# Linear attention and a Mish MLP on one core: the first 16 slots written anew

## The chip, the cores and the metric

The kernel runs on one core of a Trainium2 chip. The metric is the device time of one execution in microseconds (us), the median of several runs. A profile of one execution gives the spans of the engines: TensorE (PE, with its weight loads as PEld), VectorE (DVE), ScalarE (ACT), GpSimd (POOL) and SyncE (SP), which issues most DMAs.

## The reference

Softmax attention without a score matrix, followed by an MLP with a Mish activation, in float32:

```python
# q, k, v: (8 batches, 8 heads, 576 tokens, 64)
q_s = softmax(q, over the 64 features)
k_s = softmax(k, over the 576 tokens)
kv  = einsum('bhsd,bhse->bhde', k_s, v)      # 64 x 64 per head
att = einsum('bhsd,bhde->bhse', q_s, kv)
x   = att as (4608 tokens, 512)
h   = x @ w_in                               # 512 -> 2048
g   = h * tanh(log(1 + exp(h)))              # Mish
out = g @ w_out                              # 2048 -> 512
```

The MLP weights arrive as float64 and are converted on the chip from their two 32-bit halves.

## The kernel before

**Items and slots.** The attention is cut into 32 items of two heads each (four items per batch). An item gives `xs[i]`, 128 features of x for 512 tokens as a rounded part and a remainder, and a tail of 64 tokens that goes through DRAM. The MLP is cut into 144 slots: nine chunks of 512 tokens (eight batches and the collected tails) by 16 blocks of 128 of the 2048 hidden features. A slot `n` has an `H` part, 12 matmuls of 128x512 (four feature blocks `t` by three products of rounded parts and remainders), Mish (`Y`), a rounded copy `gh` (`G` on DVE or `GA` on ACT), a remainder `gl` (`GL`), and three slots later an `O` part of 12 matmuls into four accumulators `po`.

**Weight units.** 32 units (16 blocks of `w_in`, 16 of `w_out`) are loaded raw (`R`) and converted in steps: `RA` scales the high half on ACT into `wc`, `RL` scales the low half on ACT in place (`RM` does it on DVE), `RB` and `RC` combine the bits and the sign on DVE, `RH` rounds on ACT into the `wih` or `wo` tile, and `RO` (POOL) or `RD` (DVE) forms the remainder.

**An item, step by step.** `LQ LK L V` load q, k transposed, k and v. `MQ`, `SQ`/`SD` take q's maximum and subtract it, `EQ` is the exponential, `Q` the sums and their reciprocals, `QM`/`QD` the product. `MK`, `B` find k's maximum and bring it across the partitions by a PE transpose, `KS` subtracts, `EK` is the exponential. `K` is the `kv` product (`pkv`), `S` and `SA`/`SB` scale it into the block-diagonal 128x128 tile `kvbd`. `T` and `TC` transpose q, `X` makes `px` (512 tokens) and `pxt` (the tail), `Z`, `ZL` give `xs`, `ZT`, `ST` store the tail.

**Order.** Inside the first 16 slots the order on all engines is written out by hand in the string `FIRST`: each token is one step, and each engine executes its instructions in the order of the tokens. `STAGED` names the buffer that each raw weight unit uses. The first 16 slots contain items 0 to 7, all weight units, `H` of slots 0 to 15 and `O` of slots 0 to 12. From slot 16 on the loop `group` issues four slots at a time and one item per four slots; there items go two by two (`a_pair`, `a_kv2`, `a_x2`), with kv as 64x64 tiles in `kvt`, each product in its own quarter of the PE array.

**Memory.** PSUM has eight banks of 128x512 float32: four (`o0` to `o3`) for `po`, and for early items; two (`h`) for the `H` sums `ph`; two (`a`) for the rest. `y`, Mish's result, goes to a buffer in SBUF. `wc` has four buffers.

```python
first = FIRST.split()                       # order of the first 16 slots
...
pkv[j * D:(j + 1) * D, 0:D + 2] += r["ke"][:, c, j].T @ r["v"][:, j, c, :]
```

Of the kernel before, what the change touches and what calls it, by code (L numbers as in the profile page):

```python
# [18 lines left out]

FIRST = (  # L20
# [27 lines left out]
def attn_mish_mlp(ctx: ExitStack, tc: tile.TileContext, q, k, v, wu, qs, kt, out):  # L48
# [4 lines left out]
    HP, D = 4, v.shape[-1]  # L53
# [65 lines left out]
    def w_low(j):  # L119
        low = conv[j][0]  # L120
        nc.scalar.activation(low, low, AF.Copy, scale=0.93 * 2.0 ** -29)  # L121

    def w_low_v(j):
        low = conv[j][0]
        nc.vector.tensor_scalar(low, low, 0.88 * 2.0 ** -29, 0.45, ALU.mult, ALU.add)

    def w_bits(j):
        low, high, a = conv[j]
        nc.vector.scalar_tensor_tensor(a, a, 3, low, ALU.logical_shift_left, ALU.bitwise_or)

    def w_sign(j):
        low, high, a = conv[j]
        nc.vector.scalar_tensor_tensor(a, high, 0x80000000, a, ALU.bitwise_and, ALU.bitwise_or)
# [25 lines left out]
    vt = [p.tile([P, 2, NC + 1, D + 2], F32, tag=f"v{j}", name=f"v{j}") for j, p in enumerate((pp, pp, pp, lp))]


    for t in vt:
        nc.gpsimd.memset(t[:, :, :, D:D + 2], 1.0)
        nc.gpsimd.memset(t[ST:P, :, NC, D:D + 2], 0.0)

    def k_load(i):
        if i >= NITEM:
            return
        r = at[i] = at.get(i, {})
        t = r["k"] = (pp if i < 3 else lp).tile([P, 2, NC + 1, D], F32, tag=f"k{min(i, 3)}", name=f"k{i}")  # L170
        nc.sync.dma_start(t, k[i])  # L171
# [9 lines left out]
    def q_load(i):  # L181
        if i >= NITEM:
            return
        r = at[i] = at.get(i, {})
        if i >= COLS:
            t = r["q"] = lp.tile([P, NB, 32], F32, tag="q3", name=f"q{i}")
            nc.sync.dma_start(t, qs[i].rearrange("p (n f) -> p n f", f=32))
            return
        t = r["q"] = (pp if i < 3 else lp).tile([P, 2, NC + 1, D], F32, tag=f"q{min(i, 3)}", name=f"q{i}")
        nc.sync.dma_start(t, q[i])  # L190

    def v_load(i):
# [33 lines left out]
    def a_qmax(i):  # L226
# [21 lines left out]
    def psum(i, tag, name):  # L248

        if i < HP and tag != "a":  # L250
            return (ps_h if tag == "h" else ps_o).tile([P, 512], F32, tag=tag, name=name)
        return ps_a.tile([P, 512], F32, tag="a", name=name)

    def a_kmax(i):
        r = at[i]
        pb = ps_a.tile([P, 512], F32, tag="a", name=f"pb{i}")
# [3 lines left out]
    def a_ksub(i):  # L260
# [4 lines left out]
        nc.vector.tensor_tensor(r["k"], r["k"], mb.unsqueeze(2).to_broadcast([P, 2, NC + 1, D]), ALU.subtract)  # L265

    def a_exp(i, which="kq"):
# [3 lines left out]
        for nm in which:  # L271
            if nm == "q" and i >= COLS:
                e = r["qe"] = ap.tile([P, NB, 32], F32, tag="qe", name=f"qe{i}")
                nc.scalar.activation(e, r["q"], AF.Exp)  # L274
                continue
            if i > COLS and i % 2:
                e = pools["ke"]
            else:
                e = (pp if i in (0, 2) else ap).tile([P, NC + 1, 2, D], F32, tag=f"{nm}e", name=f"{nm}e{i}")
            nc.scalar.activation(e.rearrange("p c h d -> p h c d"), r[nm], AF.Exp)  # L280
            r[nm + "e"] = e

    def a_kv(i):
        if i >= NITEM:
            return
        r = at[i]
        pkv = psum(i, "o0", f"pkv{i}")
        for c in range(NC + 1):
            for j in range(2):
                nc.tensor.matmul(pkv[j * D:(j + 1) * D, 0:D + 2], r["ke"][:, c, j], r["v"][:, j, c, :],  # L290
                                 start=c == 0, stop=c == NC)
# [35 lines left out]
    def a_qt(i):  # L327
# [14 lines left out]
        pq = psum(i, "o1", f"pq{i}")  # L342
        for c in range(NC):
            nc.tensor.transpose(pq[:, c * P:(c + 1) * P], r["qe"][:, c].rearrange("p h d -> p (h d)"), ident)
        pq2 = psum(i, "o2", f"pqt{i}")
# [16 lines left out]
    def a_x(i):  # L362
        r = at[i]
        px = psum(i, "o3", f"px{i}")
        nc.tensor.matmul(px, kvbd[i in (1, 3) or i >= HP], r["qT"][0], start=True, stop=True)  # L365
        r["px"] = px
        a_tail1(i)
# [4 lines left out]
    def a_x2(e):  # L372
        r1, r2 = (ps_h.tile([P, 512], F32, tag="h", name=f"pt{e}_{j}") for j in range(2))
        px = [ps_a.tile([P, 512], F32, tag="a", name=f"px{e + j}") for j in range(2)]
        pt = r1[:, 0:ST], r2[:, 2 * (D + 2):2 * (D + 2) + ST]
        for dst, x in ((pt, 1), (px, 0)):
            for j in range(2):
                for h in range(2):
                    a, b = slice(h * D, (h + 1) * D), slice((h ^ j) * D, ((h ^ j) + 1) * D)
# [267 lines left out]
```

## Time and profile before

| | before |
|---|---|
| median of 3 runs | 869.4 us (868.26 to 869.88) |
| the profiled execution's own time | 868.84 us |
| its span | 867.0 us |
| granted TensorE clock, mean | 0.998 |
| PE / DVE / ACT / POOL busy | 846.7 / 474.1 / 337.1 / 92.4 us |
| DMA | 69.16 MB, 73975 packets, 52928 of them under 512 B |

How to read profile rows: a group row has the line and engine, the operation, `out<-in` with the shapes (partitions x elements), the count, then busy us and the mean ns of one, then the engine's idle time before such instructions and what ended it. A timeline row has start, length, the instruction, and in brackets the idle time before it with its releaser. `L97` is a helper that subtracts; its rows are told apart by engine and tile.

### The profile page before, as it was taken

How to read it: one execution, taken by the hardware profiler on the slowest of the kernel's cores; microseconds unless marked ns; L12 is line 12 of the kernel's file. 1: busy time of each engine (PE TensorE's matmuls, PEld its weight loads, DVE VectorE, ACT ScalarE, POOL GpSimd, SP SyncE). 2: the span in 40 equal slices, each digit the busy share in tenths (PEclk: the TensorE clock that was granted, in tenths of full speed). 3: DMA queues.
4: the chain of work that ended last, by engine and by line, in shares of the span. 5: the costliest groups of instructions: out<-in, count | busy, mean ns of one | idle time of the engine just before them, and what ended most of it. 6: DMA issues, size and time to landing. Idle time of an engine off the chain costs nothing.

```text
span 867.0 us, 11466 instructions
## 1 busy us (share of the span) xinstructions
PE 846.7 (98%) x4368; PEld 684.3 (79%) x4368; DVE 474.1 (55%) x1196; ACT 337.1 (39%) x509; POOL 92.4 (11%) x91
## 2 busy tenths in 40 slices
PE   5999999999999999999999999999999999999998
PEld 3677778787878878787878787878788788888886
DVE  7999998555574647464655656564743222222221
ACT  4999874424352434333342434243432111111111
POOL 4024221111111110111110011111110000000000
PEclk9999999999999999999999999999999999999999
DMA  9985345312321213212231223122100020001001
GB/s 307 396 263 190 106 117 136 77 28 62 92 74 46 73 48 107 62 57 63 92 77 42 69 70 83 37 62 74 62 18 1 15 73 13 1 0 50 1 1 49
DMA packets 73975, 69.16 MB, mean 80 GB/s; under 512 B 52928, under 2 KB 52928, under 8 KB 73920
## 3 DMA queue, kind: packets, MB, share of 16 engines
q1 hardware_dynamic: 73600, 67.91, 26.5%
q8 instruction: 34, 0.56, 0.3%
q10 hardware_dynamic: 320, 0.52, 0.2%
q14 instruction: 21, 0.17, 0.1%
HBM read 57.93 MB, written 10.49 MB: 79 GB/s over the span
## 4 chain that ended last, share of the span: by engine, by line
PE 89%; ACT 6%; SPq 1%; DVE 1%; issue 1%; DMA 1%; DVEq 0%; ACTq 0%
PE po L510 43%; PE ph L465 42%; PE pt L392 2%; PE px L380 1%; DMA kt<-in_kt_dram 1%; ACT L485 1%; ACT raw_out L121 1%; ACT wc_out L117 1%; ACT raw_in L121 1%; ACT y L485 0%; PE px L365 0%; ACT L280 0%; ACT wo L146 0%; SPq L171 0%; ACT wih L146 0%
## 5 line engine op out<-in xcount | busy, mean ns | idle before, releaser
L465 PE MATMUL ph<-xs,wih 128*128 128x512 f32 x1152 | 358.4, 392 | 2.5 <-ACT y L485 2.5
L510 PE MATMUL po<-wo,gh 128*128 128x512 f32 x1152 | 355.3, 389 | 0.3 <-POOL wo L97 0.3
L465 PEld LDWEIGHTS ph<-xs,wih 128*128 128x128 f32 x1152 | 213.9, 188 | 49.1 <-ACT y L485 3.8
L510 PEld LDWEIGHTS po<-wo,gh 128*128 128x128 f32 x1152 | 216.1, 188 | 45.6 <-POOL wo L97 0.6
L485 ACT ACTIVATE y<-ph 128x512 f32<-128x512 f32 x144 | 86.2, 599 | 370.0 <-PE ph L465 310.4
L465 PE MATMUL ph<-xs,wil 128*128 128x512 f32 x576 | 224.7, 390 | 0.2 <-DVE wil L97 0.2
L510 PE MATMUL po<-wo,gl 128*128 128x512 f32 x576 | 224.1, 389 | 0.0
L490 DVE CAST gh<-y 128x512 fp32r<-128x512 f32 x132 | 60.0, 455 | 270.9 <-ACT y L485 270.7
L465 PEld LDWEIGHTS ph<-xs,wil 128*128 128x128 f32 x576 | 108.1, 188 | 23.9 <-DVE wil L97 1.0
L510 PEld LDWEIGHTS po<-wo,gl 128*128 128x128 f32 x576 | 108.1, 188 | 22.5 <-DVE gl L97 0.2
L97 DVE TENSOR_TENSOR gl<-y,gh 128x512 fp32r<-128x512 f32 x144 | 100.9, 702 | 11.9
L485 ACT ACT_TABLE_LOAD x41 | 52.6, 1283 | 72.7 <-PE ph L465 72.6
L309 POOL TENSOR_TENSOR qe<-qe,qs 128x576 f32<-128x576 f32 (+1 forms) x31 | 37.0, 1192 | 304.7 <-DVE qs L304 287.1
L97 POOL TENSOR_TENSOR q<-q,qm 128x576 f32<-128x576 f32 (+1 forms) x30 | 35.8, 1194 | 198.4 <-DVE qm L224 186.5
L280 ACT ACT_TABLE_LOAD x29 | 37.2, 1283 | 6.0 <-DMA q<-in_q_dram 3.9
L300 DVE TENSOR_REDUCE qs<-qe 128x18 f32<-128x576 f32 (+1 forms) x32 | 24.6, 768 | 26.3 <-ACT qe L274 25.2
L446 DVE TENSOR_TENSOR xs<-px,xs 128x512 fp32r<-128x512 f32 x32 | 20.9, 685 | 17.0 <-ACT xs L443 17.0
L233 DVE TENSOR_REDUCE qm<-q 128x18 f32<-128x576 f32 (+1 forms) x32 | 24.4, 763 | 4.0 <-DMA q<-in_q_dram 3.7
L515 DVE COPY ob<-po 128x512 f32<-128x512 f32 x16 | 11.1, 692 | 26.7 <-PE po L510 26.7
L203 DVE TENSOR_REDUCE mxd<-kt 128x1 f32<-128x576 f32 x32 | 23.9, 746 | 0.5 <-DMA kt<-in_kt_dram 0.4
L209 DVE STREAM_TRANSPOSE mb<-mxd 32x32 f32<-32x32 f32 x96 | 19.5, 203 | 3.1
L443 ACT CAST xs<-px 128x512 fp32r<-128x512 f32 x32 | 17.7, 591 | 7.2 <-PE px L380 7.2
(94 smaller groups left out, 503.4 us busy)
## 6 DMA issues: line engine op xcount, KB each, us to landing
k<-in_k_dram SPq DMA_DIRECT2D x32, 320.0 KB, 2.9
kt<-in_kt_dram SPq DMA_DIRECT2D x32, 288.0 KB, 2.9
raw_in<-in_w_dram SPq DMA_DIRECT2D x16, 512.0 KB, 7.7
raw_out<-in_w_dram SPq DMA_DIRECT2D x16, 512.0 KB, 4.9
out_dram<-ob SPq DMA_DIRECT2D x32, 256.0 KB, 2.2
q<-in_qs_dram SPq DMA_DIRECT2D x24, 288.0 KB, 3.0
v<-in_v_dram SPq DMA_DIRECT2D x20, 320.0 KB, 4.5
v_odd<-in_v_dram SPq DMA_DIRECT2D x12, 320.0 KB, 4.6
```

Of the source, the lines that this page charges most:

```text
L97: eng.tensor_tensor(out, a, b, ALU.subtract)
L203: nc.vector.tensor_reduce(mxd, r["kt"], axis=AX.X, op=ALU.max)
L209: nc.vector.transpose(mb[h, h], mxd[h].to_broadcast([32, 32]))
L233: nc.vector.tensor_reduce(qm, qt, axis=AX.X, op=ALU.max)
L280: nc.scalar.activation(e.rearrange("p c h d -> p h c d"), r[nm], AF.Exp)
L300: nc.vector.tensor_reduce(z, q2, axis=AX.X, op=ALU.add)
L309: eng.tensor_tensor(q2, q2, z.unsqueeze(2).to_broadcast(list(q2.shape)), ALU.mult)
L446: nc.vector.tensor_tensor(xs[i][:, 1], src, xs[i][:, 0].bitcast(F32), ALU.subtract)
L465: nc.tensor.matmul(gs[n], wi[a][:, t, fs], x[:, z], start=t == 0 and i == 0, stop=t == HP - 1 and i == 2)
L485: nc.scalar.activation(y, gs[n], AF.Mish)
L490: copy(hi, gs[n])
L510: nc.tensor.matmul(po[t], g[a][:, t * P:(t + 1) * P], wo[f][:, z], start=f == 0 and i == 0, stop=f == NF - 1 and i == 2)
```

## The change

The change replaces the hand-written order of the first 16 slots and, with it, these steps:

- PSUM is one pool of eight named banks `a` to `h`. A token of `FIRST` can name its bank or banks (`H0e`, `RL2a`, `T1ae`); an `H` without one takes `g` and `h` in turn. `po` uses `a` to `d`.
- `RL` writes the scaled low half into a PSUM bank instead of in place; `RB` combines into that bank; `RC` writes the result to `wc`. `RM` is gone; all 32 units use `RL`.
- For 20 of the 32 units the rounding is a DMA issued by POOL from `wc` to the weight tile (`RI`) instead of the ACT copy (`RH`). The remainder is formed on POOL for 27 units (14 before) and on DVE for 5 (18 before).
- In the first 16 slots Mish overwrites its PSUM bank; `G`/`GA` and `GL` read it from there. `G` is on DVE 12 times and on ACT 4 times (4 and 12 before).
- Items 4 to 7 go two by two with `kvt` and 64x64 products (`KP`, `S`, `XT`, `XP`), with k's maximum and q's transposes still on PE. Each group of four heads from batch 1 on (before: batch 2) is laid out in another order.
- v is laid out with d outermost, as `[P, D + 2, 2, NC + 1]`; the `kv` matmuls read it with a step of 10 elements, and its DMA writes one contiguous run per partition. q and k have the chunk ahead of the head.
- The exponentials of items 0 to 7 are in place. `Q` is split into `Q` and `QZ`, which adds 1e-9 with an accumulator output and takes the reciprocal; `qm`, `qs`, `rs` have two buffers.
- Items 0 to 3 are taken in the order 0, 1, 3, 2 at the end of their chains, and all four `X` stand ahead of the first `H`.

The core of the diff (the new order shown by its beginning):

```diff
 FIRST = (
-    "LQ0 LK0 L0 V0 LQ1 LK1 MQ0 LQ2 MK0 SQ0 L1 B0 V1 EQ0 KS0 LK2 LQ3 Q0 EK0 L3 K0 V2 MQ1 QM0 L2 MK1 LK3 SQ1 T0 S0 V3 "
...
+    "LQ0 LK0 L0 LQ1 L1 V0 LK1 MQ0 LQ2 V1 MK0 SQ0 LQ3 LK2 B0a L2 KS0 EQ0 L3 MQ1 LK3 V2 SD1 V3 EK0 R0 Q0 R1 EQ1 K0a "
+    "LQ4 MK1 R2 QZ0 R3 Q1 QM0 B1b L4 R4 S0 MQ2 R5 SA0 T0cd R6 MQ3 SQ2 R7 R8 TC0 KS1 R9 SQ3 QZ1 EQ2 R10 X0ab MK2 R11 "
+    "EK1 R12 QM1 MK3 EQ3 R13 Q2 R14 K1c Z0 R15 Q3 ZT0 ST0 ZL0 B3b B2d S1 T1ae RL0f QZ3 SA1 QZ2 QM3 KS2 RA0 TC1 KS3 "
+    "QM2 T3cd EK2 RB0 X1ab LQ5 EK3 MQ4 RL1e RC0 SQ4 RA1 K3f TC3 RB1 RI0 K2g V4 S3 Z1 RC1 L5 SA3 T2cd ZL1 RI1 ZT1 "
+    "RA2 ST1 X3be S2 TC2 SB2 RL2a X2cd RD0 Z3 RB2 ZT3 EQ4 ST3 H0e PP ZL3 LK4 Z2 RO1 H1 V5 RC2 ZT2 RL3b ST2 ZL2 L6 "
...
+    ps = ctx.enter_context(tc.tile_pool(name="ps", bufs=1, space=bass.MemoryType.PSUM))
+    def bank(letter, name, dtype=F32):
+        return ps.tile([P, 512], dtype, tag=f"bank_{letter}", name=name)
...
-    def w_low(j):
+    def w_low(j, b):
         low = conv[j][0]
-        nc.scalar.activation(low, low, AF.Copy, scale=0.93 * 2.0 ** -29)
+        conv[j][0] = bank(b, f"low{j}", U32)
+        nc.scalar.activation(conv[j][0], low, AF.Copy, scale=0.93 * 2.0 ** -29)
...
-        nc.vector.scalar_tensor_tensor(a, a, 3, low, ALU.logical_shift_left, ALU.bitwise_or)
+        nc.vector.scalar_tensor_tensor(low, a, 3, low, ALU.logical_shift_left, ALU.bitwise_or)
...
-        nc.vector.scalar_tensor_tensor(a, high, 0x80000000, a, ALU.bitwise_and, ALU.bitwise_or)
+        nc.vector.scalar_tensor_tensor(a, high, 0x80000000, low, ALU.bitwise_and, ALU.bitwise_or)
...
+    def w_hi_dma(j):
+        a, d = w_dst(j)
+        nc.gpsimd.dma_start(d[0], a.bitcast(F32R))
...
+        t = pool.tile([P, D + 2, 2, NC + 1], F32, tag=tag, name=f"{tag}_0")
...
-                nc.tensor.matmul(pkv[j * D:(j + 1) * D, 0:D + 2], r["ke"][:, c, j], r["v"][:, j, c, :],
+                nc.tensor.matmul(pkv[j * D:(j + 1) * D, 0:D + 2], r["ke"][:, c, j], r["v"][:, :, j, c],
...
+    def a_qinv(i):
+        q2, z = at[i]["z"]
+        total = ap.tile([P, 1], F32, tag="total", name=f"total{i}")
+        nc.vector.tensor_scalar(z, z, 1e-9, 0.0, ALU.add, ALU.add, accum_out=total)
         nc.vector.reciprocal(z, z)
...
+    def a_x2(e, px, pt, order):
+        for x, j, h in order:
+            a, o = slice(h * D, (h + 1) * D), slice((h ^ j) * D, ((h ^ j) + 1) * D)
+            nc.tensor.matmul((px, pt)[x][h][o], kvt[a, j], at[e + j]["qT"][x][a], start=True, stop=True)
...
+    def g_mish0(n):
+        nc.scalar.activation(gs[n], gs[n], AF.Mish)
```

More of the change, by code (lines that the diff above doesn't have):

```diff
@@ L155, in attn_mish_mlp, with v_tile @@
     xs = {}
-    ap.tile([P, 32], F32, tag="gap0", name="gap0")
+    ap.tile([P, 96], F32, tag="gap0", name="gap0")
     xt_dram = dp.tile([B, P, HP, ST], F32, name="xt_dram")
[L159 to L164, printed above, removed]
+    def v_tile(pool, tag):
+        t = pool.tile([P, D + 2, 2, NC + 1], F32, tag=tag, name=f"{tag}_0")
+        nc.gpsimd.memset(t[:, D:D + 2], 1.0)
+        nc.gpsimd.memset(t[ST:P, D:D + 2, :, NC], 0.0)
+        return t
+    vt = [v_tile(p, f"v{j}") for j, p in enumerate((pp, pp, pp, lp))]
     def k_load(i):
@@ L246, in a_qm, with a_kmax @@
         a_qsub(i)
[L248 to L254, printed above, removed]
+    def a_kmax(i, b):
         r = at[i]
-        pb = ps_a.tile([P, 512], F32, tag="a", name=f"pb{i}")
+        pb = bank(b, f"pb{i}")
         nc.tensor.transpose(pb[:, 0:P], r["mxd"].to_broadcast([P, P]), ident)
@@ L271, in a_exp, with a_kv @@
         for nm in which:
[L272 to L277, printed above, removed]
-            else:
-                e = (pp if i in (0, 2) else ap).tile([P, NC + 1, 2, D], F32, tag=f"{nm}e", name=f"{nm}e{i}")
-            nc.scalar.activation(e.rearrange("p c h d -> p h c d"), r[nm], AF.Exp)
+            if i < COLS:
+                e = r[nm]
+            elif nm == "q":
+                e = ap.tile([P, NB, 32], F32, tag="qe", name=f"qe{i}")
+            else:
+                e = pools["ke"] if i % 2 else ap.tile([P, NC + 1, 2, D], F32, tag="ke", name=f"ke{i}")
+            nc.scalar.activation(e, r[nm], AF.Exp)
             r[nm + "e"] = e
-    def a_kv(i):
-        if i >= NITEM:
-            return
+    def a_kv(i, b):
         r = at[i]
-        pkv = psum(i, "o0", f"pkv{i}")
+        pkv = r["pkv"] = bank(b, f"pkv{i}")
         for c in range(NC + 1):
             for j in range(2):
-                nc.tensor.matmul(pkv[j * D:(j + 1) * D, 0:D + 2], r["ke"][:, c, j], r["v"][:, j, c, :],
+                nc.tensor.matmul(pkv[j * D:(j + 1) * D, 0:D + 2], r["ke"][:, c, j], r["v"][:, :, j, c],
                                  start=c == 0, stop=c == NC)
-        r["pkv"] = pkv
     def a_qsum(i):
@@ L318, in a_kvs @@
         pkv, rs = at[i]["pkv"], at[i]["rs"]
-        bd = kvbd[i in (1, 3) or i >= HP]
+        bd = kvbd[i % 2]
         for j in range(2):
@@ L360, in a_qt2, with a_x, a_xt, a_xp @@
         r["qT"] = qT, qTt
[L362 removed]
+    def a_x(i, b):
         r = at[i]
[L364 to L379, printed above, removed]
[L380 to L387 removed]
+        px, px2 = bank(b[0], f"px{i}"), bank(b[1], f"pxt{i}")
+        nc.tensor.matmul(px, kvbd[i % 2], r["qT"][0], start=True, stop=True)
+        nc.tensor.matmul(px2[:, 0:ST], kvbd[i % 2], r["qT"][1], start=True, stop=True)
+        r.update(px=px, pxt=px2[:, 0:ST])
+    def a_x2(e, px, pt, order):
+        for x, j, h in order:
+            a, o = slice(h * D, (h + 1) * D), slice((h ^ j) * D, ((h ^ j) + 1) * D)
+            nc.tensor.matmul((px, pt)[x][h][o], kvt[a, j], at[e + j]["qT"][x][a], start=True, stop=True)
+        for j in range(2):
+            at[e + j].update(dict(px=px[j]) if px else {}, **dict(pxt=pt[j]) if pt else {})
+    def a_xt(e, b):
+        a_x2(e, None, [bank(b[j], f"pt{e + j}")[:, 0:ST] for j in range(2)], [(1, j, h) for j in range(2) for h in range(2)])
+    def a_xp(e, b):
+        a_x2(e, [bank(b[j], f"px{e + j}") for j in range(2)], None, [(0, j, h) for j in range(2) for h in range(2)])
+    def a_xpair(e):
+        r1, r2 = (turn_bank(f"pt{e}_{j}") for j in range(2))
+        px = [bank("ef"[j], f"px{e + j}") for j in range(2)]
+        a_x2(e, px, (r1[:, 0:ST], r2[:, 2 * (D + 2):2 * (D + 2) + ST]),
+             [(x, j, h) for x in (1, 0) for j in range(2) for h in range(2)])
+        return r2
+    def a_kv2(e, pkv):
         for i in range(e, e + 2):
@@ L414, in a_pair @@
             a_tail3(e + 1)
-        if pkv is not None:
-            a_kvs2(f, pkv)
-    def a_tail1(i):
-        r = at[i]
-        px2 = r["pxt"] = psum(i, "a", f"pxt{i}")
-        nc.tensor.matmul(px2[:, 0:ST], kvbd[i in (1, 3) or i >= HP], r["qT"][1], start=True, stop=True)
+        if f < NITEM:
+            a_kvs2(f)
     xt_first = []
@@ L433, in a_tail2 @@
         at[i]["xt"] = xt
-        nc.scalar.copy(xt, at[i]["pxt"][:, 0:ST])
+        nc.scalar.copy(xt, at[i]["pxt"])
     def a_tail3(i):
@@ L631 @@
         "in_k_dram": rows(k, N, True),
-        "in_v_dram": rows(v, N, False),
+        "in_v_dram": rows(v, N, False).transpose(0, 1, 4, 3, 2),
         "in_w_dram": _np.ascontiguousarray(units).view(_np.int64),
```

129 lines of the change are left out of this document (69 added, 60 removed), and 36 rows, old and new, of the table FIRST.

## The prediction

> **What bounds the kernel now.** I read first the page's busy shares, then the busy time by stretch, then the PE's timeline and the chain through the end of the first 16 slots. The page:
>
> ```profile
> PE 846.7 (98%) x4368; PEld 684.3 (79%) x4368; DVE 474.1 (55%) x1196; ACT 337.1 (39%) x509; POOL 92.4 (11%) x91
> ```
>
> These are averages over stages with different limits. The busy time in three stretches (columns: stretch, its length, then busy us with counts on PE, PE's weight load, DVE, ACT, POOL, then clock, DMA share and GB/s), cut at the first `H` matmul (26.0 us) and at the first matmul of slot 16 (125.4 us):
>
> ```profile
> 0.00:26.00 26.00, 15.30 (x116) 10.87 (x117) 19.16 (x42) 15.05 (x32) 11.10 (x22) 0.93 1.01 324
> 26.00:125.40 99.40, 94.14 (x475) 72.31 (x474) 93.65 (x161) 90.31 (x161) 26.70 (x22) 1.00 0.63 207
> 125.40:310.30 184.90, 184.90 (x1027) 150.04 (x1026) 113.18 (x331) 71.48 (x96) 18.59 (x16) 1.00 0.28 76
> ```
>
> In the middle stretch three engines are nearly full at once: PE 95%, DVE 94%, ACT 91%. POOL is at 27%. After it PE alone is full, DVE at 61%, ACT at 39%. The chain and the PE timeline of that later part:
>
> ```profile
> 128.30 2.72 PE po L510 x12
> ...
> 213.91 2.96 PE ph L465 x12
> ...
> 260.12 2.96 PE ph L465 x12
> ...
> 141.83 0.81 PE L392 MATMUL pkv<-v,ke 128*64 128x66 f32 x20
> ...
> 143.15 0.73 PE L465 MATMUL ph<-xs,wih 128*128 128x512 f32 x2
> ```
>
> Twelve matmuls take 2.72 us, 227 ns each. The period of eight slots is 260.12 - 213.91 = 46.21 us, of which 16 x 2.72 = 43.52 are slot matmuls; 2.69 are one pair of items. Its `kv` half is 143.15 - 141.83 = 1.32 and the `x` half the remaining 1.37. There is no gap: what the PE has to do there sets the end. So the change can gain only ahead of 125.4 us, and it can lose behind it only by making a PE instruction slower. Every us by which slot 16 starts earlier is a us of the end.
>
> **What the middle stretch loses now.** PE timeline rows (start, length, operation, idle before and its releaser):
>
> ```profile
> 26.01 0.71 PE L465 MATMUL ph<-xs,wih 128*128 128x512 f32 x2
> ...
> 34.33 0.73 PE L465 MATMUL ph<-xs,wih 128*128 128x512 f32 x2 [1.13 <-ACT y L485]
> ...
> 55.27 0.81 PE L290 MATMUL pkv<-v,ke 128*64 128x66 f32 x20
> 56.00 0.74 PE L465 MATMUL ph<-xs,wih 128*128 128x512 f32 x2
> ...
> 61.24 0.33 PE L346 MATMUL pqt<-ident,qe 128*128 128x128 f32 x1 [1.64 <-ACT qT L358]
> ...
> 64.86 1.02 PE L365 MATMUL px<-qT,kvbd 128*128 128x512 f32 x2
> ...
> 65.85 0.70 PE L465 MATMUL ph<-xs,wih 128*128 128x512 f32 x2
> ...
> 73.87 0.60 PE L344 MATMUL pq<-ident,qe 128*128 128x128 f32 x4
> ...
> 74.33 0.71 PE L465 MATMUL ph<-xs,wih 128*128 128x512 f32 x2
> ...
> 109.91 0.73 PE L465 MATMUL ph<-xs,wih 128*128 128x512 f32 x2 [1.35 <-ACT y L485]
> ...
> 125.42 0.62 PE L465 MATMUL ph<-xs,wih 128*128 128x512 f32 x2
> ```
>
> PE's necessary work from 26.0 to 125.4: 16 `H` and 13 `O` blocks, 29 x 2.72 = 78.9. Items 4 to 7 one by one: `kv` 0.73 (56.00 - 55.27), transposes 0.46 (74.33 - 73.87), `x` with tail 0.99 (65.85 - 64.86), 2.18 each, 8.7 for four. Item 3's `x`, which lies behind the first `H`, 1.0. Sum 88.6. The stretch lasts 99.4, so 10.8 are lost: 5.3 as idle (99.40 - 94.14) and the rest in matmuls that wait for weights or run in broken sequences. Each large gap shown was ended by ACT: its queue, not its result, is late. That is what less work on ACT and DVE could give back.
>
> **The change part by part**, from rows of 0 to 125.4 us (count | busy, mean ns):
>
> ```profile
> L129 DVE SCALAR_TENSOR_TENSOR wc_out<-wc_out,raw_out 128x512 uint32<-128x512 uint32 x16 | 13.3, 856 | 0.7 <-ACT wc_out L117 0.6 <-ACT raw_out L121 0.2
> L129 DVE SCALAR_TENSOR_TENSOR wc_in<-wc_in,raw_in 128x512 uint32<-128x512 uint32 x16 | 12.7, 793 | 0.7 <-ACT raw_in L121 0.4 <-issue 0.3
> ...
> L146 ACT CAST wih<-wc_in 128x512 fp32r<-128x512 f32 x16 | 9.8, 617 | 2.5 <-DVE wc_in L133 2.5
> ...
> L121 ACT ACTIVATE raw_in<-raw_in 128x512 uint32<-128x512 uint32 x13 | 8.8, 678 | 0.0
> ...
> L97 POOL TENSOR_TENSOR wil<-wc_in,wih 128x512 fp32r<-128x512 f32 x6 | 8.1, 1356 | 16.0 <-ACT wih L146 16.0
> L280 ACT ACT_TABLE_LOAD x6 | 7.7, 1283 | 4.0 <-DMA q<-in_q_dram 3.9
> ...
> L490 ACT CAST gh<-y 128x512 fp32r<-128x512 f32 x12 | 7.3, 618 | 0.0
> ...
> L97 DVE TENSOR_TENSOR wil<-wc_in,wih 128x512 fp32r<-128x512 f32 x10 | 7.0, 707 | 1.0 <-ACT wih L146 0.8
> ...
> L446 DVE TENSOR_TENSOR xs<-px,xs 128x512 fp32r<-128x512 f32 x8 | 5.4, 679 | 0.2 <-ACT xs L443 0.2
> ...
> L323 ACT ACTIVATE kvbd<-pkv,rs 64x64 f32<-64x64 f32 x12 | 3.7, 311 | 5.2 <-DVE rs L315 5.1
> ...
> L97 DVE TENSOR_TENSOR q<-q,qm 128x640 f32<-128x640 f32 x2 | 1.6, 816 | 0.0
> ...
> L125 DVE TENSOR_SCALAR raw_in<-raw_in 128x512 uint32<-128x512 uint32 x3 | 1.3, 428 | 0.0
> ```
>
> *ACT.* The rounding of 20 of 32 weight units moves from ACT to a POOL-issued DMA (`RI` for `RH`): -20 x 0.617 = -12.3. `gh` copies on ACT fall from 12 to 4: -8 x 0.618 = -4.9. The scaled `kvbd` copies fall from 12 to 6: -6 x 0.311 = -1.9. Five `RM` become `RL` on ACT: +5 x 0.678 = +3.4. Exp and Mish alternate 14 times in the new order instead of 12: +2 x 1.283 = +2.6. Sum -13.1.
>
> *DVE.* `RD` falls from 18 to 5: -13 x 0.707 = -9.2. `RM` goes: -5 x 0.43 = -2.1. `RB` reads one operand from PSUM; its mean is stretched by POOL now, as these rows show:
>
> ```profile
> 22.31 0.69 DVE L129 SCALAR_TENSOR_TENSOR wc_in<-wc_in,raw_in 128x512 uint32<-128x512 uint32 x1
> ...
> 31.30 1.32 DVE L129 SCALAR_TENSOR_TENSOR wc_in<-wc_in,raw_in 128x512 uint32<-128x512 uint32 x1 [0.35 <-ACT raw_in L121]
> ...
> 30.77 1.30 POOL L97 TENSOR_TENSOR wil<-wc_in,wih 128x512 fp32r<-128x512 f32 x1 [8.50 <-ACT wih L146]
> ```
>
> The same instruction takes 0.69 with POOL idle and 1.32 inside a POOL subtraction. The nearest row with one SBUF and one PSUM input is `xs<-px,xs`, 0.679. I take that: -32 x (0.825 - 0.679) = -4.7; ends 0 and -5. [...] The twelve `gh` copies on DVE read PSUM now; I bound them by today's 455 ns for the SBUF form on the page and 0.692 for the `ob<-po` copy:
>
> ```profile
> L490 DVE CAST gh<-y 128x512 fp32r<-128x512 f32 x132 | 60.0, 455 | 270.9 <-ACT y L485 270.7
> ...
> L515 DVE COPY ob<-po 128x512 f32<-128x512 f32 x16 | 11.1, 692 | 26.7 <-PE po L510 26.7
> ```
>
> Taken at 0.692, the PSUM form: 12 x 0.692 - 4 x 0.455 = +6.5. Two fewer `q` products and subtractions on DVE: -1.6. The pairwise `kvbd` scaling and the accumulator outputs of `QZ` I put at +0.5 together. Sum -10.6.
>
> *POOL.* `RO` rises from 14 to 27, +13 x 1.356 = 17.6; `SQ` and `QM` gain two instructions, priced like the same subtraction, 2.7; and 20 DMA issues whose price no row shows. From 26.70 in the middle stretch POOL goes to 47.0 plus 18 issues (two lie ahead). [...] I take 1.0, so 65 of some 91 us.
>
> *PE.* Items 4 to 7 in pairs: 2 x 2.69 + 4 x 0.46 = 7.2 instead of 8.7. Item 3's `x` is ahead of the first `H` in the new order: -1.0. Necessary work 78.9 + 7.2 = 86.1.
>
> *The first `H`.* It moves behind `X2`. DVE has more ahead of it: `MQ4` and `SD1`, about 2 x 0.82, less two `RM`, 0.86; +0.8. In return the `v` loads have contiguous rows:
>
> ```profile
> k<-in_k_dram SPq DMA_DIRECT2D x32, 320.0 KB, 2.9
> ...
> v<-in_v_dram SPq DMA_DIRECT2D x20, 320.0 KB, 4.5
> ```
>
> The same 320 KB should then land in 2.9 instead of 4.5 us, and three `v` loads stand ahead of item 3's `kt` now. But DVE is busy 19.16 of the first 26 us, and its first 3.85 go to the first load, so little of it reaches the path. Against it stands `RI0`: a DMA in place of a 0.62 us cast, 1 us of issue and some 2.9 of landing, as for `k`, mostly under `X3` and `X2`. I put the first `H` at 27.0, ends 25 and 30.
>
> *Mish in PSUM, the pinned banks.* Mish, `G` and `GL` hold a bank longer, and four banks carry `ph`, `low` and items 4 to 7. No row prices it. A wait for a bank would stand on ACT's queue in front of the next Mish, for which PE waits: 0 to the whole present loss.
>
> *`v` with d outermost.* PE's streamed operand of the 320 `kv` matmuls steps 10 elements (40 bytes) instead of 1. Twenty passes of 66 columns take 0.66 us (half of 1.32) with both column halves at work together, so each half reads 66 columns per 66 ns, 1.0 a nanosecond, where a slot matmul reads 512 per 227, 2.25. A read at half rate (1.13) would still feed one half, but not two through one port. Ends: 0, and 2.0/1.13 = 1.77 times as long, +0.51 us per item. I take 0, since the stream asks for less than half of what the slot matmuls draw. [...]
>
> **Sum.** ACT falls to about 77 and DVE to 83 in the stretch, PE to 86.1: PE leads again, by little. I let half of the present loss stay, 5.4, since all three are still near 90% full and `RI` is slower than a cast. Slot 16 starts at 27.0 + 86.1 + 5.4 = 118.5 instead of 125.4: -6.9. The profiled run took 868.84 (span 867.0, 1.84 around it); 868.84 - 6.9 = 861.9. The median of the runs is 869.4, 0.6 above it. Forecast 862; with the loss at 2 and the first `H` at 25 it is 856.5, with 9 and 28 it is 866.5.
>
> **The rivals.** (1) *Strided `v`: slower.* At +0.51 per item the 24 items behind slot 16, where nothing hides PE time, cost 12.2, the eight ahead up to 4: 862 + 12.2 + 4 = 878. It passes today's time from +0.23 per item on. For it: the step; against it: the low rate of the stream. Chance 0.14.
> (2) *POOL becomes the bound.* Above (86.1 + 5.4 - 47)/18 = 2.5 us per issue POOL's in-order queue sets the pace, and `RO` behind a waiting `RI` delays weights for PE. At 3 us POOL alone needs 101 and slot 16 starts at 128: 871. Against it: 73% of POOL is free now, in waits for ACT's casts. Chance 0.14, on both sides of today's time.
> (3) *Banks take back the gain.* ACT and DVE get lighter, but waits for banks keep the loss at 10 to 11: 867 to 869. Chance 0.13; the change then hardly shows.
> (4) The forecast, 856 to 866: chance 0.59.
>
> A measurement here tells some 0.2% (1.7 us) from no change. From the cases: faster 0.68 (0.59, half of 3, a little of 2), same 0.13, slower 0.19 (most of 1, half of 2). Range 855 to 873: it holds cases 2 to 4 and leaves out strided `v` in full.
>
> **What would show it.** Slot 16's first matmul near 118.5 and the first `H` near 27; ACT and DVE below 90% between; `RB` near 0.68 with POOL busy; POOL's issues near 1 us; 46.21 us for eight slots as before, and 1.32 for a pair's `kv`. A longer period means rival 1; POOL above 90% rival 2; PE waiting for `y` while ACT waits for DVE's `gl` or `wc` rival 3.

## The result and the profile after

| | before | after |
|---|---|---|
| median | 868.83 us (868.25 to 869.88, 4 runs) | 907.47 us (905.14 to 907.74, 4 runs) |
| profiled execution, its span | 868.84, 867.0 us | 907.27, 905.5 us |
| ratio, 95% interval | | 1.0438 (1.0424 to 1.0451) |
| first `H` matmul, first matmul of slot 16 | 26.01, 125.42 us | 34.57, 149.51 us |
| period of eight slots, `kv` of a pair | 46.21, 1.32 us | 47.41, 2.53 us |

The forecast was 862 us, in the range 855 to 873. The kernel became 4.4% slower. From the page after, its span and busy shares:

```profile
span 905.5 us, 11577 instructions
...
PE 865.5 (96%) x4384; PEld 699.7 (77%) x4384; DVE 460.8 (51%) x1212; ACT 327.6 (36%) x482; POOL 123.2 (14%) x126
```

DVE and ACT have less work, as was meant, and PE is busy for longer. The same three stretches as before, cut again at the first `H` and at slot 16 (same columns):

```profile
0.00:34.57 34.57, 16.05 (x120) 11.19 (x121) 19.88 (x49) 18.03 (x38) 11.92 (x23) 0.96 0.99 365
34.57:149.51 114.94, 97.92 (x484) 74.43 (x485) 80.23 (x148) 79.72 (x128) 56.73 (x56) 0.94 0.65 192
149.51:334.40 184.89, 184.89 (x979) 150.40 (x979) 109.97 (x330) 68.00 (x91) 18.57 (x16) 1.00 0.24 71
```

In the middle stretch no engine is full any more: PE 85%, DVE and ACT 70%, POOL 49%. They wait for one another, as the list of waits below shows, and the clock is 0.94. In the last stretch PE is full and at full clock, as before. The chain there shows what has changed in it:

```profile
191.64 2.53 PE pt L416 x40
194.17 2.94 PE ph L486 x12
...
239.05 2.53 PE pt L416 x40
241.58 2.94 PE ph L486 x12
```

The slot matmuls are what they were (2.72 for twelve, 2.94 behind a pair), but the pair's `kv` takes 2.53 instead of 1.32. The period is 241.58 - 194.17 = 47.41.

So two losses add up: slot 16 starts 149.51 - 125.42 = 24.1 later, and twelve pairs behind it cost 12 x 1.21 = 14.5 more. 38.6 against the span's 905.5 - 867.0 = 38.5. Where the first of them begins is in the PE timeline and, below it, in POOL's:

```profile
27.62 0.33 PE L385 MATMUL pxt<-qT,kvbd 128*128 128x64 f32 x2
34.57 1.19 PE L486 MATMUL ph<-xs,wih 128*128 128x512 f32 x2 [6.62 <-DMA wih<-wc_in]
...
43.19 1.22 PE L486 MATMUL ph<-xs,wih 128*128 128x512 f32 x2 [5.73 <-DMA wih<-wc_in]
```

```profile
23.12 0.94 POOL L162 DMA_DIRECT2D wih<-wc_in  x1
34.75 0.77 POOL L162 DMA_DIRECT2D wih<-wc_in  x1 [10.69 <-issue]
...
43.29 2.52 POOL L111 TENSOR_TENSOR wil<-wc_in,wih 128x512 fp32r<-128x512 f32 x2 [7.49 <-DMA wih<-wc_in]
```

`RI0` is issued at 23.12, before anything waits for it, and `H0` can start only at 34.57: the rounding landed 11.3 us after its issue. DVE's timeline has `RC1`, which makes the second unit's `wc`, at 24.28, over at 24.95; yet `RI1` is issued at 34.75, when the first rounding is through, after 10.69 us that the profile puts down to nothing but the issue itself. PE then waits a second time. The DMAs issued from 20 to 50 us, and the landing times of all `wih` roundings before slot 16:

```profile
GB/s 399 412 392 410 425 393 404 426 404 393 372 385 382 391 380 396 393 407 427 399 415 426 426 399 396 336 340 372 356 352 390 394 351 293 44 10 0 82 268 358
...
raw_in<-in_w_dram SPq DMA_DIRECT2D x4, 512.0 KB, 11.6
wih<-wc_in POOLq DMA_DIRECT2D x3, 256.0 KB, 8.4
```

```profile
DMA to landing us min/median/max: 2.8/5.3/11.3
```

The DMA engines move 336 to 427 GB/s until 44 us, with the raw weights themselves landing only 11 to 12 us after their issue. The rounding is one more transfer among these. Who waits for whom up to slot 16, the largest of the waits (us in total, times, longest):

```profile
POOL wil L111 <- DMA wih<-wc_in: 16.9, 5, 7.5
PE ph L486 <- DMA wih<-wc_in: 14.1, 3, 6.6
POOL wo L111 <- DMA wo<-wc_out: 12.2, 6, 3.1
POOL wih L162 <- issue: 10.7, 1, 10.7
...
ACT wc_in L131 <- POOL wil L111: 8.2, 4, 4.7
DVE wil L111 <- DMA wih<-wc_in: 8.0, 1, 8.0
ACT low L136 <- DVE xs L467: 7.5, 1, 7.5
```

This is a ring: POOL waits for the rounding before it can subtract, a `wc` buffer comes free only with that subtraction, and ACT waits for the buffer before it can scale the next unit. The last two lines show that the first rounding held more than PE. `RD0`, the remainder of unit 0, needs it too, and stands in DVE's order ahead of `RB2`, `ZL3` and the rest: DVE did nothing from 26.43 to 34.46. ACT then stood for 7.5 us, since `RL3` writes to the PSUM bank that `ZL3` (`xs`, L467) has to read first. In the profile before, most of PE's idle time between the first `H` and slot 16 was ended by ACT, 4.6 of 5.1 us.

### The profile page after: what moved, and what is told of

Same layout as the page of the kernel before. It is cut to its first block, busy times and chain, and to the rows that moved or that the text cites. A ratio compares the mean times of both kernels' runs of the same rounds, so it can differ in the third digit from the quotient of the medians.

```text
span 905.5 us, 11577 instructions
## 1 busy us (share of the span) xinstructions
PE 865.5 (96%) x4384; PEld 699.7 (77%) x4384; DVE 460.8 (51%) x1212; ACT 327.6 (36%) x482; POOL 123.2 (14%) x126
## 4 chain that ended last, share of the span: by engine, by line
PE 85%; DMA 1%; issue 1%; DVE 0%; POOL 0%; ACT 0%; POOLq 0%
PE po L534 40%; PE ph L486 40%; PE pt L416 3%; PE px L394 1%; DMA wo<-wc_out 1%; PE pt L394 0%; PE pkv L416 0%; POOL wo L111 0%; DVE gl L111 0%; PE pq L363 0%; DVE wo L111 0%; DVE wc_out L144 0%; DVE gh L514 0%; ACT ob L539 0%; POOL wil L111 0%
## 5 line engine op out<-in xcount | busy, mean ns | idle before, releaser
L509 ACT ACTIVATE y<-ph 128x512 f32<-128x512 f32 x128 | 76.7, 599 | 374.1 <-PE ph L486 314.6
L514 DVE CAST gh<-y 128x512 fp32r<-128x512 f32 x128 | 57.2, 447 | 272.9 <-ACT y L509 272.7
L111 DVE TENSOR_TENSOR gl<-y,gh 128x512 fp32r<-128x512 f32 x128 | 89.4, 698 | 12.2 <-DVE gh L514 0.5
L328 POOL TENSOR_TENSOR qe<-qe,qs 128x576 f32<-128x576 f32 x24 | 27.9, 1161 | 305.6 <-DVE qs L324 305.6
L314 DVE TENSOR_REDUCE qs<-qe 128x18 f32<-128x576 f32 x24 | 18.1, 752 | 25.2 <-ACT qe L297 25.2
L467 DVE TENSOR_TENSOR xs<-px,xs 128x512 fp32r<-128x512 f32 x32 | 20.7, 685 | 16.5 <-ACT xs L464 16.5
L111 POOL TENSOR_TENSOR wil<-wc_in,wih 128x512 fp32r<-128x512 f32 x15 | 19.3, 1289 | 18.9 <-DMA wih<-wc_in 16.9
```

What stands on the lines that cost most here:

```text
L111: eng.tensor_tensor(out, a, b, ALU.subtract)
L328: eng.tensor_tensor(q2, q2, z.unsqueeze(2).to_broadcast(list(q2.shape)), ALU.mult)
L467: nc.vector.tensor_tensor(xs[i][:, 1], src, xs[i][:, 0].bitcast(F32), ALU.subtract)
L509: nc.scalar.activation(y, gs[n], AF.Mish)
L514: copy(hi, gs[n])
```

## The experiments

Each ratio is against the kernel before on the same chip, with its 95% interval; the starts are those of the profiled execution.

### The strided v

**The kernel before with v laid out d outermost, nothing else** (`e6`):

```diff
-    vt = [p.tile([P, 2, NC + 1, D + 2], ...
+    vt = [p.tile([P, D + 2, 2, NC + 1], ...
-    nc.tensor.matmul(pkv[...], r["ke"][:, c, j], r["v"][:, j, c, :], ...
+    nc.tensor.matmul(pkv[...], r["ke"][:, c, j], r["v"][:, :, j, c], ...
```

> The kernel before with only v's layout changed to d outermost (step 10, contiguous runs of 2560 bytes in its DMA). Theory C: eight slots 47.4 us, 12 pairs cost 14.5 us, items 4 to 7 ahead of slot 16 up to 2.4 more, less up to 2 for earlier v loads: 882 to 886 us. Rival (the pairs' kv is slower for another reason of the new kernel): 868.

882.15 us, 1.0158 (1.0143 to 1.0173). Its chain:

```profile
166.09 2.53 PE pt L392 x40
168.62 2.94 PE ph L465 x12
...
213.50 2.53 PE pt L392 x40
216.03 2.94 PE ph L465 x12
```

The layout alone makes 2.53 of 1.32. Slot 16 starts at 123.93, 1.5 earlier than before, because contiguous v lands sooner (median 3.4 instead of 4.5 us; first `H` at 25.18). -1.5 + 14.5 = +13.0; the span grew from 867.0 to 879.9. The eight items ahead of slot 16 cost nothing that shows.

**Which steps cost.** Two layouts between, with all roundings on ACT (see `e1`). For PE only the step differs; the runs of v's DMA are shorter too. `e7` has the two heads innermost, a step of 2 elements (8 bytes); `e8` the chunks innermost, 5 elements (20 bytes):

```diff
-        t = pool.tile([P, D + 2, 2, NC + 1], ...     # r["v"][:, :, j, c]
+        t = pool.tile([P, NC + 1, D + 2, 2], ...     # e7: r["v"][:, c, :, j]
+        t = pool.tile([P, 2, D + 2, NC + 1], ...     # e8: r["v"][:, j, :, c]
```

> As the kernel with all casts on ACT, v laid out [chunk, d, head]: step 2 (8 bytes), DMA runs of 512 bytes. [...] Theory C2 (any step halves PE's read rate): 2.5 us, 884. Theory C3 (the cost grows with the step): in between, 872 to 880.

> [...] Theory C3: in between, 874 to 881 us.

`e7`: 873.06 us, 1.0053 (1.0038 to 1.0068). `e8`: 886.54 us, 1.0207 (1.019 to 1.0224). A pair's `kv` in the chain, first of `e7`, then of `e8`:

```profile
145.26 1.36 PE pkv L416 x40
```

```profile
145.10 2.55 PE pkv L416 x40
```

Steps of 1, 2, 5 and 10 elements take 1.32, 1.36, 2.55 and 2.53 us. It is not a slope: there are two levels, and the edge lies between 8 and 20 bytes; steps of 12 and 16 bytes were not run. A price for any step other than 1 would have put 2 elements near 2.53, and one that grows with the bytes between two elements would have put 10 well above 5. (The time of `e7` alone, 873.06, would fit the expectation C3; it is the 1.36 that decides against it and against C2, and its first `H` is late, at 30.47 where `e1` has 29.03. `e8` is above the range that C3 gives it.) Why the edge lies there, no run shows.

**The changed kernel with v read in rows, step 1** (`e3`): the tile is `[P, NC + 1, 2, D + 2]`, read as `r["v"][:, c, j, :]`; its DMA writes rows of 64 elements.

> The changed kernel with v's tile laid out [chunk, head, d], so that the kv matmuls read it with step 1; its DMA then writes runs of 256 bytes. Theory C (the 40-byte step slows PE's stream): a pair's kv takes 1.32 us instead of 2.53, eight slots 46.2 instead of 47.4, 12 pairs give 14.5 us: 893 us, slot 16 within 2 us of 149.7. Rival (something else of the pairs has become slower): 905 or more and 2.5 us kv as before.

898.21 us, 1.0344 (1.0327 to 1.0361). The `kv` is back at 1.32, and 9.3 us are gained, not 14.5: slot 16 starts at 154.71, 5.2 later than after, with the first `H` at 37.27. In short rows v lands later (median of five loads in the first 40 us: 7.4 us, 6.5 after), so longer runs do help the loads. Two layouts have longer runs without a wide step for PE:

**The kernel before with step 2** (`e12`), and **with rows of 66 that bring their two columns of ones from device memory** (`e11`, step 1, whole runs, no fill on the chip):

```diff
-        nc.sync.dma_start(t[:, :, :, 0:D], v[i])
+        nc.sync.dma_start(t[:, :, 0:D], v[i])        # e12, t: [P, NC + 1, D + 2, 2]
+        nc.sync.dma_start(t, v[i])                   # e11, v[i] has D + 2 columns
```

> The kernel before with v as [chunk, d, head]: step 2, runs of 512 bytes. By the step-2 run with casts a pair's kv takes 1.37 instead of 1.32 (12 x 0.05 = 0.6 us), and the DMA gains about half of what full runs gain: 867 to 868.5 us.

> The kernel before with v stored with its two columns of ones: the gain of the contiguous DMA without the strided read. The strided form started the first H 0.8 us and slot 16 1.5 us earlier although its kv took 0.6 us longer four times: slot 16 at 121.5 to 123.5 instead of 125.4, 864.5 to 866.5 us against 868.3. Rival (the earlier loads are lost in ACT's and DVE's queues): 868.

`e12`: 867.96 us, 0.9984 (0.9976 to 0.9993). `e11`: 867.89 us, 0.9992 (0.9983 to 1.0001). The first `H` starts at 24.97 and 25.09 instead of 26.01, slot 16 at 124.66 and 124.80. `e12` is the one version here that beats the kernel before clear of the noise, by 0.16%; `e11` can't be told from it, so the rival of its expectation held: most of what the earlier loads gain is lost on the way.

### The rounding by DMA

**All 20 roundings back on ACT** (`e1`), and **only the first two** (`e2`), v still strided:

```diff
-    "... RB1 RI0 K2g ... ZL1 RI1 ZT1 ..."
+    "... RB1 RH0 K2g ... ZL1 RH1 ZT1 ..."     # e2; e1: every RI<j> becomes RH<j>
```

> The changed kernel with all 20 rounding DMAs (RI) back as ACT casts (RH) at the same places of the order. Theory A (the roundings by POOL-issued DMA land late and hold PE ahead of slot 16): first H near 28 us instead of 34.6, no wait of PE for a DMA of wih or wo, slot 16 starts at 122 to 130 us instead of 149.7, so about 880 to 886 us. Theory B (the new order and the pinned banks are what costs): slot 16 stays at 145 or later, over 900 us. The 47.4 us for eight slots stays either way.

> The changed kernel with only the first two roundings (units 0 and 1) back as ACT casts. Theory A1 (the loss is that the first two DMAs are issued while the DMA engines are full of weight loads: 11.3 us to landing, and the second issue waits for the first): first H near 28, the later DMAs cost little, slot 16 at 130 to 135, so about 888. Theory A2 (each rounding DMA costs, early or late): slot 16 only 6 to 9 us earlier, 897 to 900. Theory B: no change of more than 3 us.

`e1`: 885.92 us, 1.0201 (1.0186 to 1.0216), slot 16 at 128.16. `e2`: 894.71 us, 1.0305 (1.0287 to 1.0323), slot 16 at 137.41. So of the 24.1 us by which slot 16 was late, 21.4 are the roundings: 12.1 the first two, the rest the other 18, about half a us each. `e2` lies between its two expectations: both the early roundings and the later ones cost.

The first two cost PE more than the waits. With the clock beside it (PE, weight load, DVE, ACT, POOL busy, then clock), PE's start after:

```profile
34.57:38.00 3.43, 2.90 (x6) 1.75 (x6) 3.40 (x6) 1.49 (x3) 0.99 (x3) 0.50 1.02 412
38.00:43.19 5.19, 0.00 (x0) 0.00 (x0) 2.54 (x7) 1.89 (x4) 0.00 (x0) 0.50 1.17 363
43.19:49.00 5.81, 5.60 (x13) 3.97 (x14) 1.89 (x3) 1.19 (x2) 5.71 (x6) 0.51 0.52 173
49.00:60.00 11.00, 11.00 (x53) 9.11 (x52) 8.25 (x14) 9.98 (x17) 5.94 (x6) 1.00 0.57 177
```

The first wait, 6.6 us, leaves the granted clock at half, and it stays there through 3.43 us of work and the second wait, 5.7, until 5.7 us into the work behind it. 2.90 + 5.60 us of matmuls ran at about half speed (483 and 431 ns each, where a slot matmul takes 227), so about 4.2 us were lost in matmuls that wait for nothing. Cut finer, the trace has the clock at half from 31.78 to 48.84, which is five steps of 3.41. PE did nothing in the step ahead, 28.37 to 31.78, and was busy for 0.62, 2.28, 0.00, 2.03 and 3.41 us of the five; the clock came back behind the only one that it filled. A step ahead of half clock is not always idle throughout: in the profile before, one with 1.95 us of PE work, 17.25 to 20.66, is followed by 3.41 us at half clock. In `e2` the clock over the middle stretch is 0.98. With the first `H` 34.57 - 29.09 = 5.5 earlier and the second wait gone, these 4.2 are part of the 12.1.

**A larger `dynamic_dma_scratch_size`** (`e4`), to see why `RI1` is issued so late:

```diff
-    nc = _bacc.Bacc(..., dynamic_dma_scratch_size=1024)
+    nc = _bacc.Bacc(..., dynamic_dma_scratch_size=1536)
```

> The changed kernel with 1536 instead of 1024 bytes per partition kept for the descriptors of POOL-issued DMAs. Theory A3 (POOL's second DMA is not issued until the first has drained, since the space for descriptors is full: in the changed kernel its operand was ready at 25.0 us, it was issued at 34.8): the second issue comes at about 25 us, both land by 36 to 40, slot 16 starts 4 to 8 us earlier, 898 to 902 us. Rival (the space isn't what holds it): second issue at 34 to 35 us as before, 907 us.

```profile
25.23 0.75 POOL L162 DMA_DIRECT2D wih<-wc_in  x1 [1.20 <-DVE wc_in L144]
```

`RI1` now goes out as soon as `RC1` is done, at 25.23 instead of 34.75, 9.5 us earlier: the size of this space had held POOL. That it is descriptors that fill it is the expectation's account; the runs show the two times. But the second rounding lands only 14.8 us later, at 40.0, and the time is 904.77 us, 1.0417 (1.0399 to 1.0435), which overlaps the changed kernel's interval. The second wait shrinks from 5.73 to 2.54 and slot 16 starts 2.9 earlier, less than the 4 to 8 expected, while the first `H` stays at 34.58 and the clock is still at half until 46 us. It also falls to half for 3.41 us three more times behind 70 us, which it did not after, so the 2.9 are not the price of the blocked issue alone. Freeing the issue gives little of the 24.1 back.

**The loads of units 4 to 15 issued later** (`e9`), behind `ST3`, to see whether the landing is long because the DMA engines are full:

```diff
-    "... R3 Q1 QM0 B1b L4 R4 S0 MQ2 R5 ... Q2 R14 K1c Z0 R15 ... EQ4 ST3 H0e ..."
+    "... R3 Q1 QM0 B1b L4 S0 MQ2 ... Q2 K1c Z0 ... EQ4 ST3 R4 R5 ... R15 H0e ..."
```

> The changed kernel with the raw loads R4 to R15 moved in SP's order to behind ST3, so that the first two rounding DMAs meet DMA engines with little queued. Theory A1 (these DMAs are slow because they share the engines with a deep queue of weight loads): the first lands in 3 to 4 us instead of 11.3, the first H starts at 28 to 30 us instead of 34.6 and the second wait of 5.7 is below 2; the later weight units then come late, so the time may fall little or rise: 895 to 915. Rival (a cast of 512-byte rows by a POOL-issued DMA takes 8 us or more by itself): landing at 8 us or more, first H at 33 or later.

POOL's issues and DVE's first subtraction (durations, then first and last start):

```profile
23.79 0.93 POOL L140 DMA_DIRECT2D wih<-wc_in  x1
28.65 0.76 POOL L140 DMA_DIRECT2D wih<-wc_in  x1 [3.93 <-issue]
```

```profile
L89 DVE TENSOR_TENSOR wil<-wc_in,wih x1: 693/693/693, 28.4 to 28.4; 128x512 fp32r<-128x512 f32 x1
...
DMA to landing us min/median/max: 4.5/5.8/10.9
```

The same rounding now lands 4.5 us after its issue instead of 11.3, and the first `H` starts at 28.47, right behind the matmul ahead of it. So the long landing is contention with the weight loads. The time is 901.47 us, 1.0374 (1.036 to 1.0388): 6 us of the 38 come back. The experiment isn't clean, since weights that are loaded later are also late themselves; and the second rounding, issued at 28.65 behind the first, still makes PE wait, for 4.21 (below 2 was expected). Behind that wait the clock is at half until 40.97, and for 3.41 us four more times ahead of slot 16.

**Where the other 18 cost.** On top of `e10` (below: ACT rounds, v in rows of 66) the DMA rounding is put back for nine middle units, 4, 5, 8, 10, 11 and 14 to 17 (`e14`), or for nine late ones, 21 to 29 (`e13`):

```diff
-    "... H9 RH4 R16 ... RH5 ... R19 RH8 ..."
+    "... H9 RI4 R16 ... RI5 ... R19 RI8 ..."          # e14, and so on to RI17
-    "... H40g RB22 RH21 ... RB23 RH22 ..."
+    "... H40g RB22 RI21 ... RB23 RI22 ..."            # e13, and so on to RI29
```

> The same with the DMA roundings for units 4 to 17 (nine) and casts for the others. Theory A1: these carry the cost, 877 to 881 us. Theory A2: 875 to 877, as with the late ones.

> As the changed kernel with padded v (step 1), roundings by POOL-issued DMA only for units 21 to 29 (nine), the other eleven back on ACT. Against all casts on ACT (871.4 us, slot 16 at 128.1): theory A1 (these DMAs cost only while the engines are full of weight loads): 869 to 872, the nine casts off ACT's 88.6 us bring it to 83. Theory A2 (each costs about half a us, since POOL's own subtraction waits for it and holds the wc buffer): 875 to 877.

`e14`: 881.44 us, 1.0136 (1.0119 to 1.0153). `e13`: 874.36 us, 1.006 (1.0045 to 1.0075). Against `e10` (871.38) the middle nine cost 10.1 us, the late nine 3.0. How long the roundings took to land, `e14` first:

```profile
wo<-wc_out POOLq DMA_DIRECT2D x5, 256.0 KB, 5.9
...
wih<-wc_in POOLq DMA_DIRECT2D x4, 256.0 KB, 6.7
```

```profile
wo<-wc_out POOLq DMA_DIRECT2D x5, 256.0 KB, 2.8
wih<-wc_in POOLq DMA_DIRECT2D x4, 256.0 KB, 4.3
```

The nine whose roundings take longer to land cost more; they are issued from 35 to 86 us, while the DMA engines move 278 GB/s, the others from 84 to 116, at 159. The landing is not all of it: ahead of slot 16 the clock is at half for 10.2 us in `e14` and 6.8 in `e13`, in `e10` never, and up to half of that, 5.1 and 3.4, can be lost by it. `e13` came out between its two expectations. Nor do the two add up to the 8.8 us that all 18 cost by `e2` and `e1` (894.71 - 885.92): 10.1 + 3.0 is more. Those two runs have v strided and 3.4 us each at half clock, so the clock is not in their difference. What one late rounding costs by its landing alone was not isolated.

### What the new order is worth

**Both repaired in the simple way** (`e5`): `e1` and `e3` together.

> The changed kernel with all 20 roundings as ACT casts and v with step 1: the new order, the banks and the pairs of items 4 to 7 alone. If the two parts add up (18.5 us from the casts, 9 from v): 880 us. Theory D (v's short runs cost 3 us ahead of the first H only because the POOL-issued DMAs wait behind them): with casts that goes away, eight slots 46.2, slot 16 at 126 to 128: 868 to 871. If the new order by itself gains: below 866.

874.75 us, 1.007 (1.0055 to 1.0085), which lies between its two expectations; the two causes explain all but 0.7%. The first `H` is at 31.87, with v in short rows.

**Both repaired, v in rows of 66** (`e10`): `e5` with v's two columns of ones in device memory, as in `e11`.

> The changed kernel with casts on ACT and v stored in device memory with its two columns of ones, rows of 66: step 1 for PE and one run of 2640 bytes per partition for the DMA. Against the same with 256-byte runs (874.8 us, first H at 31.9): first H at 29, slot 16 at 128 less 2.4 of the strided kv, about 870. If the new order gains anything once both parts are repaired: below 866.

871.38 us, 1.0033 (1.002 to 1.0047). The middle stretch and PE's largest waits in it:

```profile
29.26:128.10 98.84, 90.97 (x486) 70.10 (x486) 78.99 (x149) 88.56 (x149) 43.84 (x34) 1.00 0.57 196
```

```profile
PE ph L485 <- DVE kvt L424: 2.2, 1, 2.2
PE pb L275 <- ACT xt_first L454: 1.7, 1, 1.7
PE px L393 <- DVE ke_odd L283: 1.2, 1, 1.2
```

Here everything else of the change is in force: low halves and Mish in PSUM, items 4 to 7 in pairs, DVE at 79.0 instead of 93.7 us. ACT, with the casts back, is at 88.6 and was at 90.3. PE's own work fell by 94.14 - 90.97 = 3.2 us, and its idle time rose from 5.3 to 7.9. The stretch is 98.8 long instead of 99.4, and starts 3.25 later. So the order with the casts on ACT gains nothing: the waits are others, for banks and steps of the items.

**One of those waits removed** (`e15`): in `e10` an `H` stands in bank `g`, which is free only after `S4`, the scaling that empties it. `S4` moves directly behind `KP4`:

```diff
-    "... MQ7 KP4g RL16h RB15 SQ7 RA16 G6 RA17 L7 S4 RO14 ..."
+    "... MQ7 KP4g S4 RL16h RB15 SQ7 RA16 G6 RA17 L7 RO14 ..."
```

> As the changed kernel with padded v and all casts on ACT, the step S4 (scaling of the kv of items 4 and 5, which frees PSUM bank g) moved on DVE's queue to directly behind KP4. Theory E (PE waits at H28g for the bank that S4 reads: 2.18 us with the release by the kvt instruction): that wait falls below 0.5 us and slot 16 starts 1.5 to 2 us earlier, 869.5 to 870. Rival (ACT and DVE take it back later, their queues set the pace): the wait goes, slot 16 stays within 0.5 us of 128.1, 871.

871.21 us, 1.0027 (1.0015 to 1.0039), no change, with slot 16 at 129.01:

```profile
PE ph L463 <- DVE kvt L402: 1.4, 1, 1.4
...
PE ph L463 <- DVE wc_in L122: 0.8, 1, 0.8
```

The wait became 1.4, not below 0.5, and a new one of 0.8 for `wc_in` stands beside it, so neither expectation held in full. Making one wait shorter moved the next one in. What else holds the order back was not tried.

## Why the prediction was wrong, step by step

**The sum with measured terms.** The forecast was 861.9, with slot 16 at 118.5. The order alone (`e10`, casts on ACT) has it at 128.1: +9.6, of which 2.3 is the first `H` (29.26, not 27.0) and 7.3 the stretch (98.8, not 86.1 + 5.4). The roundings add 149.51 - 128.10 = 21.4 (`e1`, with the step still in, gives the same), the strided v 14.5 behind slot 16. 861.9 + 9.6 + 21.4 + 14.5 = 907.4; the profiled execution took 907.27. That the sum closes says only that no stretch is left out; what each part is rests on its runs.

**Failed: "I take 0" for v with d outermost.** Measured +0.605 per item (half of 1.21), above the upper end of 0.51, which is rival 1 in kind. The argument was that a stream that asks for less than half of what a slot matmul draws would hide a read at half rate. That set one column half, 1.0 column a nanosecond, against a slot matmul's 2.25. Both halves together, which the prediction puts at 2.0 when it works out the upper end, draw 0.89 of it, so there was nothing to hide behind. The half rate of 1.13 was an estimate of the author's that no row stood behind; measured with the step are 40 x 66 columns in 2.53 us, 1.04 a nanosecond for both halves together, and 20 bytes (2.55 us) cost as much as 40. No row spoke for the 0, so a range between 0 and 0.51 should not have been closed at one end. Rival 1's other half, up to 4 us for the eight items ahead of slot 16, was wrong: `e1` and `e10` have slot 16 at 128.2 and 128.1, with and without the step.

**Failed: "some 2.9 of landing, as for `k`, mostly under `X3` and `X2`".** The 2.9 was a median over the `k` loads of the whole run, most of them in its quiet part. The profile before had the right price, in the same view cut to 20 to 50 us:

```profile
raw_in<-in_w_dram SPq DMA_DIRECT2D x7, 512.0 KB, 9.4
...
k<-in_k_dram SPq DMA_DIRECT2D x1, 320.0 KB, 9.3
```

With 9.3 in place of 2.9, 6.4 more, the first `H` would have been put at up to 33, above the upper end of 30. The rounding landed after 11.3, and `X2` ended at 27.95, so 6.6 were open. With it came effects that the prediction had no term for: DVE held for 8.0 us by `RD0` and ACT for 7.5 behind it, the second issue held until the first was through (`e4`), and the clock at half for 8.5 us of matmuls.

**Failed: the other 18 priced by POOL's time alone.** The issue's price, taken as 1.0, stood on no run; the runs showed 0.79 us for `wih` and 0.57 for `wo`. It was near, and POOL is 49% busy, so rival 2's bound was not reached. Its second half, subtractions behind a waiting rounding, is what happened. Landing time is no one's busy time, but it holds a `wc` buffer, and the ring POOL, ACT, DVE runs at its pace. These rows show the prices:

```profile
L162 POOL DMA_DIRECT2D wih<-wc_in x10 | 7.9, 789 | 12.5 <-issue 10.7 <-DVE wc_in L144 1.8
...
L162 POOL DMA_DIRECT2D wo<-wc_out x10 | 5.7, 574 | 7.0 <-DVE wc_out L144 6.0 <-ACT low L136 1.0
```

**Failed: "I let half of the present loss stay".** Rival 3 was nearer: by `e10` none of the loss came back, though not for the bank waits that it named alone. There DVE is less busy, 80% instead of 94, and PE waits no less. ACT is as full there as before, 90%; what a lighter ACT is worth without the waits for the roundings, no run shows.

**Right: most prices of single instructions.** `RB` into PSUM takes 0.69, beside POOL too (0.686 to 0.697 in the seven inside a POOL subtraction; 0.679 was taken), `gh` from PSUM 0.688 (0.692), and the tables are loaded 14 times. DVE's busy time up to slot 16 fell by 112.8 - 100.1 = 12.7 (10.6 was forecast). ACT's fell by 105.4 - 97.8 = 7.6, though its rows in the view by lines add up to 119.4 and 105.7, which is 13.7 less (13.1 was forecast): busy time counts an overlap of two instructions once, and that is 14.0 us before and 7.9 after. Two rows of the new prices:

```profile
L140 DVE SCALAR_TENSOR_TENSOR low<-wc_in,low 128x512 uint32<-128x512 uint32 x16 | 11.1, 691 | 9.6 <-ACT wc_in L131 7.1 <-ACT low L136 2.2
...
L514 DVE CAST gh<-ph 128x512 fp32r<-128x512 f32 x11 | 7.6, 688 | 5.2 <-ACT ph L505 5.2
```

The signals that the prediction named for the profile after told the rivals apart: a longer period meant rival 1, and it came; POOL above 90% didn't. ACT and DVE below 90%, named as a sign of the forecast, came as well, with the time far above it: it says that they have less to do, not that PE waits less.

## What to carry to other kernels

A cast moved to a DMA is gone from the engine's queue, but not from the path: price it by the landing times of transfers in the same stretch, with every engine whose next instruction waits for it, the buffers that it holds, and the clock that PE loses while it waits (here the first two, 0.62 us each on ACT, cost 12.1). A layout that makes a DMA contiguous can cost the matmul that reads it more than it saves (here 14.5 us against 1.5); look at the bytes between two elements of the streamed operand. When three engines are each nearly full, taking work off one of them may only exchange the waits (in `e10` DVE's busy time fell by 14.7 us, and PE's idle time rose by 2.6), so test the order by itself before the rest is built on it.

## What was not expected of the hardware

- The cost of a strided read by PE had two levels at the four steps that were run, not a slope: 40 passes of 66 columns took 1.32, 1.36, 2.55 and 2.53 us at steps of 4, 8, 20 and 40 bytes.
- The same 256 KB rounding DMA took from 2.8 to 11.3 us to land; the first one took 11.3, and 4.5 with the weight loads issued later (`e9`). With a `dynamic_dma_scratch_size` of 1024 POOL issued the second one at 34.75, when the first was through; with 1536 at 25.23.
- The granted clock was at half for 3.41 us before and for five times that after. After waits of 6.6 and 5.7 us the matmuls ran at 0.50 until 5.7 us into the work, when PE had filled one whole step of 3.41; a step with 1.95 us of work was followed by half clock too.
- ACT wrote the scaled low half, 128x512, a little faster into PSUM than into SBUF: 0.63 us instead of 0.67 to 0.68.
